# Which transposes go through the DMA crossbar: the folded weights in place of normalised tokens and attention outputs

## The chip, the cores and the metric

The kernel runs on one core of one Trainium2 chip. The metric is the device time of one execution in microseconds. Before the change three executions took 206.52, 206.75 and 206.77 us, a median of 206.75 us.

## The reference

One layer norm feeds two branches, and their outputs are added to the input:

```
xn  = layernorm(x)                       # x: 2048 tokens x 512
q,k,v = split(xn @ wqkv)                 # 32 heads of 16
phi(t) = [softmax(t @ w_phi), softmax(-t @ w_phi)]   # per head, 32 features
kv  = phi(k)^T v ;  z = sum over tokens of phi(k)
o   = (phi(q) kv) / (phi(q) z + 1e-6)
h   = xn @ w1 + b1 ;  act = h * tanh(softplus(h))    # 1792 wide
out = x + o @ wo + act @ w2
```

All tensors are bf16. The attention has no causal mask: kv and z are sums over all tokens, so no o can be made before every token's k and v are done.

## The kernel before, in words

The 2048 tokens are four groups (g) of four tiles (t) of 128 tokens. The width 512 is four blocks of 128 (kt, or j on the head side). TensorE contracts over the partitions, so everything that enters a matmul as a contraction needs its contracted axis on the partitions: the normalised tokens as `xnT` (width on the partitions), the attention output as `oT` (heads on the partitions).

**Loads (lines 69 to 93).** Two queues issue them: ScalarE's queue takes `wk_raw` (L73), `Wsrc` (L77) and `wq_raw` (L81); SyncE's queue takes the first token group in two halves (L71, L74), `wv`, `b1row`, the two halves of `w1_sb` (L86, L87), token group 1 (L89), `w2_sb` (L91) and `wo_sb` (L93). A DMA that ScalarE issues holds ScalarE for the length of the issue. The framework gives DMAs one of eight completion semaphores in turn; a ninth DMA waits, in its queue, for the one that had the semaphore before. L87 is the one that shares with L73.

**Fold (`fold`, L218 to L246).** w_phi is applied to wk and wq once: `wkp = wk @ blockdiag(w_phi)`, and `wqp` likewise. For each of the two, 16 TensorE transposes (L225) put the weight's columns on the partitions in two PSUM banks `ptrw`, two ScalarE copies (L231) take them to `wT`, and 16 small matmuls (L236) against `Wbd` make the folded weight, a bank `pf` for each kt; the banks are copied out by VectorE (L244, even kt) and ScalarE (L246, odd kt).

**Layer norm (`stage_ln`, L166 to L205).** VectorE takes statistics (L178, L179), ScalarE the square root (L182), VectorE the reciprocal (L186) and the normalised tile `xn` (L188). For group 0 TensorE transposes `xn` (L200) into PSUM banks `ptr`, and ScalarE copies them to `xnT` (L204). For groups 1 to 3 the transpose is a DMA (L197) on SyncE's queue, one for each tile, from SBUF to SBUF.

**First loop over the groups (L445 to L462).** `stage_kv_pair`: keys `pk` (L253), two exponentials `ek` (L261, L262), values `pv` (L267), the softmax sums `ss` (L275), reciprocals (L281), and the weighted values `v12` (L283, L291). `stage_q`: queries `pq` (L328), exponentials `eq` (L336, L337), then for each of eight slices a matmul `pS` (L342) and a VectorE product `eqT` (L349). The next group's tokens are loaded (L459) and normalised. `stage_kvacc`: 32 matmuls `pkv` (L303), accumulated by VectorE (L311, L313). `stage_h`: 56 matmuls `ph` (L364) and 14 activations (L374).

**Second loop (L478 to L480).** `stage_o`: for each tile 8 matmuls `pnd` (L388), a reciprocal (L397) and a product `o_t` (L399), which a DMA transpose on SyncE's queue brings into `oT` (L405). `stage_out`: for each tile 14 matmuls with the MLP activations (L415) and 4 with `oT` (L423) in one bank `po`, the addition of x (L431) and the store (L432).

**What sets the order.** Each engine runs its instructions in a fixed order that a scheduler made when the program was built; it interleaves stages (matmuls `ph` fill the time in which VectorE works on the softmax). `chain` fixes the order of ScalarE's activations, and with it the table loads. PSUM has three pools of two buffers: `kq` (pk, pq, ph, pnd), `v` (pv, po), `m` (ptr, ptrw, pf, pS, pkv). The token pool `xg` has two buffers.

Of the kernel before, what the change touches and what calls it, by code (L numbers as in the profile page):

```python
# [8 lines left out]
BF16 = mybir.dt.bfloat16  # L9
# [8 lines left out]
def kernel(  # L18
# [50 lines left out]
    xgs[0] = xpool.tile([P, TPG, D], BF16, name="xg")  # L69
    x0 = x2[0 : TPG * P].rearrange("(t p) d -> p t d", p=P)  # L70
    nc.sync.dma_start(xgs[0][:, 0:2, :], x0[:, 0:2, :])  # L71
    wk_raw = prep_w.tile([P, KT, D], BF16, name="wk_raw")
    nc.scalar.dma_start(wk_raw[:], wqkv_v[:, :, D : 2 * D])  # L73
    nc.sync.dma_start(xgs[0][:, 2:4, :], x0[:, 2:4, :])  # L74
    Wsrc = prep_w.tile([P, 4, DH], BF16, name="Wsrc")
    with nc.allow_non_contiguous_dma(reason="tiny w_phi load"):
        nc.scalar.dma_start(Wsrc[:], wphi_v)  # L77
    wv = wts.tile([P, KT, D], BF16, name="wv")
    nc.sync.dma_start(wv[:], wqkv_v[:, :, 2 * D : 3 * D])
    wq_raw = prep_w.tile([P, KT, D], BF16, name="wq_raw")  # L80
    nc.scalar.dma_start(wq_raw[:], wqkv_v[:, :, 0:D])  # L81
    b1row = prep_w.tile([FT, P], BF16, name="b1row")
    nc.sync.dma_start(b1row[:], b1_v)
    w1_sb = wts.tile([P, KT, F], BF16, name="w1_sb")
# [81 lines left out]
    def stage_ln(g):  # L166
        xg = xgs[g]
        mv = spool.tile([P, TPG, nc.vector.BN_AGGR_DIM], FP32, name="mv")
        rstd = spool.tile([P, TPG], FP32, name="rstd")
        xnT = xnTpool.tile([P, TPG, KT, P], BF16, name="xnT")  # L170
        step = 1 if g == 0 else TPG
        for t0 in range(0, TPG, 2):
            ptr = bank_m("ptr", [P, 2, KT, P], BF16) if g == 0 else None
            for t in range(t0, t0 + 2):
                if t % step == 0:
                    for u in range(t, t + step):
                        st = spool.tile([P, nc.vector.BN_STATS_DIM], FP32, name="st")
                        nc.vector.bn_stats(st[:], xg[:, u, :])  # L178
                        nc.vector.bn_aggr(mv[:, u, :], st[:])  # L179
                    us = slice(t, t + step)  # L180
                    chain(
                        nc.scalar.activation(  # L182
                            rstd[:, us], mv[:, us, 1], ACT.Sqrt, bias=eps_t[:]
                        )
                    )
                    nc.vector.reciprocal(rstd[:, us], rstd[:, us])  # L186
                xn = xnpool.tile([P, D], BF16, name="xn")
                nc.vector.tensor_scalar(  # L188
                    out=xn[:],
                    in0=xg[:, t, :],  # L190
                    scalar1=mv[:, t, 0:1],
                    scalar2=rstd[:, t : t + 1],
                    op0=ALU.subtract,
                    op1=ALU.mult,
                )
                if g > 0:
                    nc.sync.dma_start_transpose(out=xnT[:, t], in_=xn[:])  # L197
                    continue
                for kt in range(KT):
                    nc.tensor.transpose(  # L200
                        ptr[:, t - t0, kt, :], xn[:, kt * P : (kt + 1) * P], ident[:]
                    )
            if g == 0:
                nc.scalar.copy(xnT[:, t0 : t0 + 2], ptr[:])  # L204
        return xnT  # L205


# [7 lines left out]
        op=ALU.mult,  # L215
    )

    def fold(src, dst):  # L218
        wTs = []
        for jh in range(2):  # L220
            ptr = bank_m("ptrw", [P, 2, 512], BF16)
            for jj in range(2):
                j = 2 * jh + jj
                for kt in range(KT):
                    nc.tensor.transpose(  # L225
                        ptr[:, jj, kt * P : (kt + 1) * P],
                        src[:, kt, j * P : (j + 1) * P],
                        ident[:],
                    )
            wT = prep_w.tile([P, 2, 512], BF16, name="wT", bufs=2)  # L230
            nc.scalar.copy(wT[:], ptr[:])  # L231
            wTs.append(wT)
        for kt in range(KT):
            pf = bank_m("pf")
            for j in range(4):
                nc.tensor.matmul(  # L236
                    pf[:, j * P : (j + 1) * P],
                    lhsT=wTs[j // 2][:, j % 2, kt * P : (kt + 1) * P],
                    rhs=Wbd[:, j, :],
                    start=True,  # L240
                    stop=True,
                )
            if kt % 2 == 0:
                nc.vector.tensor_copy(dst[:, kt, :], pf[:])  # L244
            else:
                nc.scalar.copy(dst[:, kt, :], pf[:])  # L246


    def stage_kv_pair(xnT, pr):
        pk = big("pk")  # L250
        for tt in range(2):
            for kt in range(KT):
                nc.tensor.matmul(  # L253
                    pk[:, tt, :],
                    lhsT=xnT[:, 2 * pr + tt, kt, :],
                    rhs=wkp[:, kt, :],
                    start=(kt == 0),
                    stop=(kt == KT - 1),
                )
        ek = ekpool.tile([P, 2, 2, 512], BF16, name="ek")  # L260
        chain(nc.scalar.activation(ek[:, 0], pk[:], ACT.Exp))  # L261
        chain(nc.scalar.activation(ek[:, 1], pk[:], ACT.Exp, scale=-1.0))  # L262
        v12s = []
        for tt in range(2):
            pv = bank_v("pv")
            for kt in range(KT):
                nc.tensor.matmul(  # L267
                    pv[:],
                    lhsT=xnT[:, 2 * pr + tt, kt, :],
                    rhs=wv[:, kt, :],  # L270
                    start=(kt == 0),
                    stop=(kt == KT - 1),
                )
            ss = spool.tile([P, 2, NH], FP32, name="ss")
            nc.vector.reduce_sum(  # L275
                ss[:],
                ek[:, :, tt, :].rearrange("p s (h e) -> p s h e", e=DH),
                axis=AX.X,
            )
            rk = spool.tile([P, 2, NH], FP32, name="rk")  # L280
            nc.vector.reciprocal(rk[:], ss[:])  # L281
            v12 = vpool.tile([P, 2, NH, VW], BF16, name="v12")
            nc.vector.tensor_tensor(  # L283
                out=v12[:, :, :, 0:DH],
                in0=pv[:]
                .rearrange("p (o h e) -> p o h e", o=1, e=DH)
                .to_broadcast([P, 2, NH, DH]),
                in1=rk[:, :, :, None].to_broadcast([P, 2, NH, DH]),
                op=ALU.mult,
            )  # L290
            nc.gpsimd.tensor_copy(v12[:, :, :, DH], rk[:])  # L291
            v12s.append(v12)
        return ek, v12s
# [27 lines left out]
    def stage_q(g, xnT):  # L321
        gs = slice(g * 512, (g + 1) * 512)
        for jp in range(2):
            pq = big("pq")
            for jj in range(2):
                j = 2 * jp + jj
                for kt in range(KT):
                    nc.tensor.matmul(  # L328
                        pq[:, jj, :],
                        lhsT=wqp[:, kt, j * P : (j + 1) * P],  # L330
                        rhs=xnT[:, :, kt, :],
                        start=(kt == 0),
                        stop=(kt == KT - 1),
                    )
            eq = eqpool.tile([P, 2, 2, 512], BF16, name="eq")
            chain(nc.scalar.activation(eq[:, 0], pq[:], ACT.Exp))  # L336
            chain(nc.scalar.activation(eq[:, 1], pq[:], ACT.Exp, scale=-1.0))  # L337
            for jj in range(2):
                j = 2 * jp + jj
                for pl in range(2):  # L340
                    pS = bank_m("pS")
                    nc.tensor.matmul(  # L342
                        pS[:],
                        lhsT=B16b[:],
                        rhs=eq[:, 1 - pl, jj, :],
                        start=True,
                        stop=True,
                    )
                    nc.vector.tensor_tensor(  # L349
                        out=eqT[:, pl * 4 + j, gs],  # L350
                        in0=pS[:],
                        in1=eq[:, pl, jj, :],
                        op=ALU.mult,
                    )


    def stage_h(xnT, pool):
        act = pool.tile([P, FT, 512], BF16, name="act")
        for fp in range(FT // 2):
            ph = big("ph")  # L360
            for ff in range(2):
                f = 2 * fp + ff
                for kt in range(KT):
                    nc.tensor.matmul(  # L364
                        ph[:, ff, :],
                        lhsT=w1_sb[:, kt, f * P : (f + 1) * P],
                        rhs=xnT[:, :, kt, :],
                        start=(kt == 0),
                        stop=(kt == KT - 1),
                    )  # L370
# [8 lines left out]


    def stage_o(g):
        oT = oTpool.tile([P, TPG, 4, P], BF16, name="oT")
        for t in range(TPG):
            tok0 = g * 512 + t * P
            pnd = big("pnd")
# [16 lines left out]
                in1=rd[:, :, :, None].to_broadcast([P, 2, 16, DH]),  # L402
                op=ALU.mult,
            )
            nc.sync.dma_start_transpose(out=oT[:, t], in_=o_t[:])  # L405
        return oT

    def stage_out(g, act, oT):
        xg2 = xpool.tile([P, TPG, D], BF16, name="xg")
        nc.sync.dma_start(xg2[:], x_g[g])  # L410
        for t in range(TPG):
# [10 lines left out]
            for j in range(4):  # L422
                nc.tensor.matmul(  # L423
                    po[:],
                    lhsT=oT[:, t, j, :],
                    rhs=wo_sb[:, j, :],
                    start=False,
                    stop=(j == 3),
# [8 lines left out]
    chain(nc.scalar.activation(warm[:], eps_t[:], ACT.Sqrt))  # L437
    xnTs[0] = stage_ln(0)
    chain(nc.scalar.activation(warm[:], eps_t[:], ACT.Exp))
    fold(wk_raw, wkp)  # L440
    fold(wq_raw, wqp)
    pb = bank_m("pb", [P, FT], BF16)
    nc.tensor.transpose(pb[:], b1row[:], ident[0:FT, 0:FT])
    nc.vector.tensor_copy(b1f[:], pb[:])
# [66 lines left out]
```

## Time and profile before

| what | value |
|---|---|
| median of three executions | 206.75 us |
| the profiled execution | 206.77 us |
| its span in the trace | 205.1 us |
| TensorE matmul busy | 185.3 us |
| VectorE busy | 117.3 us |
| ScalarE busy | 91.4 us |
| granted TensorE clock | 0.999 |

The profile is of one execution. Its span runs from the first to the last instruction; 1.7 us of the execution lie outside. Times in the trace count from the span's start. TensorE's matmuls are pipelined, so that a 128x512 matmul is listed with 379 ns, but eight in a row take 1.73 us; what a matmul costs its queue is the distance to the next, 0.216 us, and not its listed duration. A row for a DMA on a queue shows the time in which the queue was held by the issue; the landing is listed apart.

### The profile page before, as it was taken

The page shows a single profiled execution, that of the slowest core. Times are in us where ns is not written, and L with a number is a line of the kernel's source. Part 1 is how long each engine was busy: PE and PEld are TensorE (multiplying, and loading weights), DVE is VectorE, ACT ScalarE, POOL GpSimd, SP SyncE. Part 2 cuts the span into 40 slices and gives each one's busy share as a digit, 9 for nine tenths or more (in the row PEclk, how much of TensorE's full clock was granted, in tenths as well). Part 3 has the DMA queues.
Part 4 walks back from the last instruction along what each step waited for, and adds up shares of the span by engine and source line. Part 5 has one row for each costly group of instructions (what it writes and reads, how often), then busy time and mean ns, then how long its engine had stood idle before and what let it go on. Part 6 is the DMA issues. An engine that isn't in the chain of part 4 may idle for free.

```text
span 205.1 us, 2739 instructions
## 1 busy us (share of the span) xinstructions
PE 185.3 (90%) x1073; PEld 92.5 (45%) x1073; DVE 117.3 (57%) x205; ACT 91.4 (45%) x119; POOL 8.6 (4%) x25
## 2 busy tenths in 40 slices
PE   0396999999888999989999999999999999999993
PEld 0264443554333644336443446544544464455441
DVE  1807699971999903999309987261372154127211
ACT  2574998448985278994498743600000000000000
POOL 2000011000111000110001100000000000000000
PEclk9999999999999999999999999999999999999999
DMA  5999600084000182000440000053072127103310
GB/s 165 341 372 348 213 0 0 2 80 128 0 2 0 26 94 88 0 0 3 77 128 0 0 3 2 0 102 54 26 198 58 52 69 165 51 29 77 76 51 26
DMA packets 27320, 15.92 MB, mean 78 GB/s; under 512 B 16300, under 2 KB 27308, under 8 KB 27308
## 3 DMA queue, kind: packets, MB, share of 16 engines
q1 hardware_dynamic: 25724, 14.69, 28.0%
q10 hardware_dynamic: 1584, 1.07, 1.8%
q8 instruction: 8, 0.13, 0.2%
q14 instruction: 4, 0.03, 0.1%
HBM read 9.98 MB, written 2.10 MB: 59 GB/s over the span
## 4 chain that ended last, share of the span: by engine, by line
PE 52%; DVE 22%; DMA 13%; ACT 6%; issue 5%; SPq 1%; ACTq 0%
PE po L415 21%; PE ph L364 11%; PE po L423 7%; DMA xg<-in_A_x_dram 7%; DVE eqT L349 5%; DVE ss L275 5%; DMA oT<-o_t 4%; DVE st L178 3%; PE pk L253 3%; PE pv L267 3%; PE pnd L388 2%; DMA wk_raw<-in_A_wqkv_dram 2%; DVE xn L188 2%; ACT ek L262 2%; PE pkv L303 2%
## 5 line engine op out<-in xcount | busy, mean ns | idle before, releaser
L364 PE MATMUL ph<-xnT,w_sb 128*128 128x512 bf16 x224 | 55.0, 379 | 0.5 <-ACT act L374 0.5
L415 PE MATMUL po<-w_sb,act 128*128 128x512 bf16 x224 | 52.4, 379 | 0.0
L374 ACT ACTIVATE act<-ph,b1f 128x512 bf16<-128x512 f32 x56 | 35.2, 684 | 27.5 <-PE ph L364 27.5
L431 DVE TENSOR_TENSOR y<-po,xg 128x512 bf16<-128x512 f32 x16 | 11.1, 692 | 43.4 <-PE po L423 43.3
L364 PEld LDWEIGHTS <-w_sb 128*128 128x128 bf16 x224 | 21.6, 98 | 27.2 <-issue 3.1
L415 PEld LDWEIGHTS <-act 128*128 128x128 bf16 x224 | 21.5, 98 | 23.6
L275 DVE TENSOR_REDUCE ss<-ek 128x64 f32<-128x1024 bf16 x16 | 18.7, 1200 | 16.7 <-ACT ek L262 16.7
L349 DVE TENSOR_TENSOR eqT<-pS,eq 128x512 bf16<-128x512 f32 x32 | 20.5, 685 | 1.1 <-PE pS L342 0.9
L178 DVE BATCH_NORM_STATS2 st<-xg 128x6 f32<-128x512 bf16 x16 | 10.4, 673 | 15.1 <-DMA xg<-in_A_x_dram 15.1
L267 PE MATMUL pv<-wv,xnT 128*128 128x512 bf16 x64 | 16.6, 385 | 1.4 <-DVE v_594 L283 1.4
L423 PE MATMUL po<-wo_sb,oT 128*128 128x512 bf16 x64 | 16.5, 379 | 0.9 <-DMA oT<-o_t 0.9
L328 PE MATMUL pq<-xnT,wqp 128*128 128x512 bf16 x64 | 15.1, 379 | 1.6 <-ACT ek L262 1.5
L253 PE MATMUL pk<-wkp,xnT 128*128 128x512 bf16 x64 | 15.8, 379 | 0.0
L342 PE MATMUL pS<-eq,B16b 128*128 128x512 bf16 x32 | 11.6, 378 | 1.1 <-DVE eqT L349 1.1
L399 DVE TENSOR_TENSOR o_t<-pnd,rd 128x512 bf16<-128x512 f32 x16 | 11.1, 692 | 0.5
L328 PEld LDWEIGHTS <-wqp 128*128 128x128 bf16 x64 | 6.2, 97 | 9.7 <-issue 2.8
L267 PEld LDWEIGHTS <-xnT 128*128 128x128 bf16 x64 | 6.3, 100 | 8.5 <-issue 1.9
L423 PEld LDWEIGHTS <-oT 128*128 128x128 bf16 x64 | 6.0, 98 | 9.1 <-DMA oT<-o_t 2.2
L388 PEld LDWEIGHTS <-eqT 128*128 128x128 bf16 x128 | 8.2, 98 | 3.8 <-DVE o_t L399 2.3
L200 PE MATMUL ptr<-ident,xn 128*128 128x128 bf16 x16 | 2.0, 311 | 8.7 <-DVE xn L188 8.7
L388 PE MATMUL pnd<-kvm,eqT 128*128 128x136 bf16 x128 | 9.6, 223 | 0.0
L261 ACT ACTIVATE ek<-pk 128x1024 bf16<-128x1024 f32 x8 | 8.2, 1029 | 2.3 <-ACT ek L262 2.1
(99 smaller groups left out, 171.6 us busy)
## 6 DMA issues: line engine op xcount, KB each, us to landing
xg<-in_A_x_dram SPq DMA_DIRECT2D x7, 512.0 KB, 3.8
out_dram<-y SPq DMA_DIRECT2D x16, 128.0 KB, 1.7
w_sb<-in_B_w_dram SPq DMA_DIRECT2D x2, 896.0 KB, 9.1
w_sb<-in_B_w_dram SPq DMA_DIRECT2D x1, 1792.0 KB, 14.7
wk_raw<-in_A_wqkv_dram ACTq DMA_DIRECT2D x1, 512.0 KB, 4.8
xg<-in_A_x_dram SPq DMA_DIRECT2D x2, 256.0 KB, 4.4
wv<-in_A_wqkv_dram SPq DMA_DIRECT2D x1, 512.0 KB, 7.5
wq_raw<-in_A_wqkv_dram ACTq DMA_DIRECT2D x1, 512.0 KB, 8.4
```

The lines of the kernel that those rows point to most:

```text
L178: nc.vector.bn_stats(st[:], xg[:, u, :])
L253: nc.tensor.matmul(pk[:, tt, :], lhsT=xnT[:, 2 * pr + tt, kt, :], rhs=wkp[:, kt, :], start=(kt == 0), stop=(kt == KT - 1),)
L267: nc.tensor.matmul(pv[:], lhsT=xnT[:, 2 * pr + tt, kt, :], rhs=wv[:, kt, :], start=(kt == 0), stop=(kt == KT - 1),)
L275: nc.vector.reduce_sum(ss[:], ek[:, :, tt, :].rearrange("p s (h e) -> p s h e", e=DH), axis=AX.X,)
L328: nc.tensor.matmul(pq[:, jj, :], lhsT=wqp[:, kt, j * P : (j + 1) * P], rhs=xnT[:, :, kt, :], start=(kt == 0), stop=(kt == KT - 1),)
L342: nc.tensor.matmul(pS[:], lhsT=B16b[:], rhs=eq[:, 1 - pl, jj, :], start=True, stop=True,)
L349: nc.vector.tensor_tensor(out=eqT[:, pl * 4 + j, gs], in0=pS[:], in1=eq[:, pl, jj, :], op=ALU.mult,)
L364: nc.tensor.matmul(ph[:, ff, :], lhsT=w1_sb[:, kt, f * P : (f + 1) * P], rhs=xnT[:, :, kt, :], start=(kt == 0), stop=(kt == KT - 1),)
L374: nc.scalar.activation(act[:, f, :], ph[:, ff, :], ACT.Mish, bias=b1f[:, f : f + 1])
L388: nc.tensor.matmul(pnd[:, j // 2, (j % 2) * 136 : (j % 2) * 136 + 136], lhsT=eqT[:, pl * 4 + j, tok0 : tok0 + P], rhs=kvm[:, pl * 4 + j, : ...
L415: nc.tensor.matmul(po[:], lhsT=act[:, f, ts], rhs=w2_sb[:, f, :], start=(f == 0), stop=False,)
L423: nc.tensor.matmul(po[:], lhsT=oT[:, t, j, :], rhs=wo_sb[:, j, :], start=False, stop=(j == 3),)
```

## The change

The crossbar transposes move from the activations to the weights. `wkT` and `wqT` are loaded already transposed, each by one DMA transpose of 512x512 from DRAM on ScalarE's queue, in the place where `wk_raw` and `wq_raw` were loaded. `fold` keeps only its matmuls and the copies of `pf`. The tiles of groups 1 to 3 are now transposed as those of group 0 were: 16 TensorE transposes a group into two banks of the pool `m`, and two ScalarE copies of 128x1024. The attention output likewise: 16 TensorE transposes a group into two banks `ptro` of the same pool, and two ScalarE copies into `oT`. The layouts of `xnT` and `oT` change from (tile, block, 128) to (block, 512).

```diff
-    nc.scalar.dma_start(wk_raw[:], wqkv_v[:, :, D : 2 * D])
+    wkT = prep_w.tile([P, 4, D], BF16, name="wkT")
+    nc.scalar.dma_start_transpose(out=wkT[:], in_=A_wqkv[:, D : 2 * D])
...
-    nc.scalar.dma_start(wq_raw[:], wqkv_v[:, :, 0:D])
+    wqT = prep_w.tile([P, 4, D], BF16, name="wqT")
+    nc.scalar.dma_start_transpose(out=wqT[:], in_=A_wqkv[:, 0:D])
...
         for t0 in range(0, TPG, 2):
-            ptr = bank_m("ptr", [P, 2, KT, P], BF16) if g == 0 else None
+            ptr = bank_m("ptr", [P, KT, 2 * P], BF16)
...
-                if g > 0:
-                    nc.sync.dma_start_transpose(out=xnT[:, t], in_=xn[:])
-                    continue
                 for kt in range(KT):
                     nc.tensor.transpose(
-                        ptr[:, t - t0, kt, :], xn[:, kt * P : (kt + 1) * P], ident[:]
-                    )
-            if g == 0:
-                nc.scalar.copy(xnT[:, t0 : t0 + 2], ptr[:])
+                        ptr[:, kt, (t - t0) * P : (t - t0 + 1) * P],
+                        xn[:, kt * P : (kt + 1) * P],
+                        ident[:],
+                    )
+            nc.scalar.copy(xnT[:, :, t0 * P : (t0 + 2) * P], ptr[:])
...
-    def fold(src, dst):
-        wTs = []
-        for jh in range(2):
-            ptr = bank_m("ptrw", [P, 2, 512], BF16)
...
-            wT = prep_w.tile([P, 2, 512], BF16, name="wT", bufs=2)
-            nc.scalar.copy(wT[:], ptr[:])
-            wTs.append(wT)
+    def fold(wT, dst):
...
-            nc.sync.dma_start_transpose(out=oT[:, t], in_=o_t[:])
+            o_ts.append(o_t)
+        for jh in range(2):
+            ptr = bank_m("ptro", [P, 2, 512], BF16)
+            for t in range(TPG):
+                for jj in range(2):
+                    j = 2 * jh + jj
+                    nc.tensor.transpose(
+                        ptr[:, jj, t * P : (t + 1) * P],
+                        o_ts[t][:, j * P : (j + 1) * P],
+                        ident[:],
+                    )
+            nc.scalar.copy(oT[:, 2 * jh : 2 * jh + 2, :], ptr[:])
```

## The prediction

> **What bounds the kernel now.** First the page's head and its first part, then the chain of waits in order of time, to see where TensorE sets the pace and where something else does.
>
> ```profile
> span 205.1 us, 2739 instructions
> PE 185.3 (90%) x1073; PEld 92.5 (45%) x1073; DVE 117.3 (57%) x205; ACT 91.4 (45%) x119; POOL 8.6 (4%) x25
> PE   0396999999888999989999999999999999999993
> ```
>
> TensorE is busy almost throughout, except in the first four slices (20 us). The chain tells which parts are TensorE's. In it, columns are start, length, and work:
>
> ```profile
> 6.02 10.00 DMA xg<-in_A_x_dram
> 16.04 0.69 DVE st L178
> ...
> 18.63 0.46 PE ptrw L225 x8
> ...
> 23.67 1.22 DVE ss L275
> ...
> 46.69 3.53 DMA xg<-in_A_x_dram
> 50.24 1.29 DVE st L178 x2
> ...
> 75.48 1.73 PE pk L253 x8
> ```
>
> Two DMA arrivals hold VectorE: token group 1 at 16.04 us, and token group 3 at 50.24 us, whose load stands in SyncE's queue behind the four crossbar transposes of group 1 (held 40.68 to 46.64 by the timeline). Eight matmuls of 512 columns take 1.73 us, 0.216 each; eight warm transposes take 0.46, 0.058 each. From the timeline the stages are: start to the first softmax sum `ss` 23.67 us; from there to group 1's first `pk` at 46.09, 22.42; group 1 to 75.31, 29.22; group 2 to 102.92, 27.61; group 3 to 130.91, 27.99; outputs to 201.67, 70.76; tail 3.40. Their sum is 205.07.
>
> TensorE's work in a group is 112 x 0.216 + 32 x 0.06 (`pkv`) = 26.1 us, in an output group 72 x 0.216 + 32 x 0.058 (`pnd`) = 17.4. So group 2 has 1.5 us of gaps, group 1 3.1, the four output groups together 2 (the first lacks four `po`, done earlier). The extra 1.6 of group 1 is VectorE's late statistics: `ss` comes 4.75 us after `pk` in group 2, 6.9 in group 1.
>
> **What the Trainium skill says.** "Perfetto Trace Analysis", Per-instruction lifecycle (HWDGE): the slot of a DMA on its queue is descriptor generation; moving the data is not in it. The trace agrees:
>
> ```profile
> L405 SPq DMA_TRANSPOSE oT<-o_t x16: 1189/1208/1225, 132.5 to 189.8; - x16
> DMA to landing us min/median/max: 2.4/2.4/3.9
> ```
>
> The queue is held 1.21 us, the data land 2.4 us after the issue. "DMA: Bandwidth & Descriptors", Latency and other measured facts, gives 261 GB/s for a crossbar transpose: 2.0 us for one 512 KB weight. The trace has no transpose from DRAM; from SBUF its 256-byte packets took 18 ns (median), so 16 engines need 2048 x 18 / 16 = 2.3 us, against 1.5 for 512 packets of 1024 bytes at 46 ns. I take 2.3. "TensorE: Matmul & The Clock Gate", Part 4, gives about 275 ns for a transpose in context; here 219 is what one lasts, 0.058 us what one costs in a row; the measurement decides.
>
> ```profile
> L225 PE MATMUL ptrw<-ident,wq_raw 128*128 128x128 bf16 x16 | 1.1, 219 | 0.0
> L204 ACT COPY xnT<-ptr 128x1024 bf16<-128x1024 bf16 x2 | 1.9, 1004 | 0.0
> L423 PE MATMUL po<-wo_sb,oT 128*128 128x512 bf16 x64 | 16.5, 379 | 0.9 <-DMA oT<-o_t 0.9
> ```
>
> The last row shows what the removed transposes of `o_t` cost TensorE: 0.9 us in all.
>
> **The change part by part.** TensorE loses 32 transposes and gains 48 + 64: +80 x 0.058 = +4.6 us on an engine that is nearly full. What the rest adds or gives back, stage by stage:
>
> *Start.* Gone are 32 transposes (1.9 us) and four ScalarE copies (4 x 1.0), which lie on the chain. But in the built program VectorE's order is `wkp` twice, then the first statistics of group 1, then `wqp`. VectorE waits there for group 1's tokens, and TensorE's later `pf`, the eighth `pk` and `ek` wait for `wqp`'s bank. Counting on: statistics 0.69, `wqp` 0.69, `pf` and last `pk` about 0.6, ScalarE's last `wqp` copy 0.6, two `ek` 2.05, with hand-overs: `ss` starts 4.8 us after the tokens land. They land at 16.04 now. The two weights cost the DMA engines 2 x (2.3 - 1.5) = 1.6 us more ahead of them, and the second half of `w1_sb`, which stands ahead of them in the queue, waits for `wkT`:
>
> ```profile
> SPq L87 <- DMA wk_raw<-in_A_wqkv_dram: 2.3, 1, 2.3
> ```
>
> I take a landing at 17.6 to 18, so `ss` at 22.6.
>
> The other limit is ScalarE's issue. Not shown: what a 512x512 transpose from DRAM holds. Low bound: a plain load's 0.49 us, and ScalarE is free at 2.45 as now. High bound: four times 1.21, twice, from 0.81, with `Wsrc` between: free at 11.1. Behind it stand the square roots of group 0. From a free ScalarE to `ss` I count 12.0 us: table load 1.28, four roots with VectorE's `xn` to 3.8, transposes to 4.2, two copies to 5.9 (after the second table load), then the `pf` banks, two at a time, each through a copy of 0.6 to 0.7: `wqp` done at 9.9, two `ek` 2.05. That gives `ss` at 14.5 or 23.1. The later limit decides: 22.6 to 23.1. I take 22.7, 1.0 earlier than now.
>
> *Group 0, from `ss`.* In the built program it has the order that group 2 has now, where `ss` to next `pk` takes 102.92 - 80.06 = 22.9. Added: 16 transposes 0.93; VectorE's one statistics of group 2 before `xn`, 0.2 of its 0.69 after cover by `ph`; and waits in pool `m`: `pkv`'s banks must wait for ScalarE's copies of `ptr` (2 x 1.0 after the eighth transpose), of which the remaining transposes and three `ph` hide all but 0.5. 24.5 us, +2.1. Without that `ph` cover the copies would cost about 1.1 more.
>
> *Group 1.* Group 2's 27.6 + 0.93 + 0.5 = 29.0: -0.2. The 1.6 goes, since group 3's load no longer stands behind transposes: it issues when group 1's `xn` are done (about 40) and lands 3.8 later, ahead of its statistics. What is late next is `ek`, as in group 2.
>
> *Group 2.* The same sum, 29.0: +1.4. *Group 3* has no transposes: 0.
>
> ScalarE's copies (2.0 a group) lie in its waits for `ph` (27.5 us over the loop). The copies of `oT` fall where ScalarE has nothing: its slices are zero from 133 us on.
>
> *Outputs.* 64 x 0.058 = +3.7. The 0.9 of waits for DMA goes. Transposes of `o_t` wait for VectorE, but in places where `pnd` waited for the same `o_t` already, so they fill about 0.2 a group. New: the fourth tile's transposes end, ScalarE copies `ptro` twice (2.0), while TensorE has five `po`, two `po` with `oT`, two `po`: 1.9. About 0.3 a group stays. Sum 3.7 - 0.9 - 0.6 + 1.2 = +3.4. If the nine matmuls did not cover the copies, each group would lose 1.9 more.
>
> SyncE's queue is only relieved: 28 transposes leave it, and stores and loads behind them go earlier; no one waits for those.
>
> Sum: -1.0 + 2.1 - 0.2 + 1.4 + 0 + 3.4 = +5.7, span 210.8. The profiled execution took 206.77 for a span of 205.1, so 1.7 lie around it, and it is 0.02 above the median: 212.5 us.
>
> **The rivals.**
> *(a) The crossbar load is slow from DRAM.* Twice 18 ns per packet is 9.2 us of all engines for both weights instead of 3.0 in the plain loads: tokens of group 1 at 22.2, `ss` at 27.0, 4.3 later than forecast: 216.8 us. For it: one packet of a queue takes its turn against one of the other, and the transposed weight comes in four times as many. Against it: the engines have only 3.4 MB to bring in that time.
> *(b) The start gains more and the banks cost nothing.* Landing at 16.04, `ss` at 20.9 (-1.8), no waits in pool `m` (-1.5), 0.6 less in the outputs: 208.6 us. Still slower: the transposes are TensorE work.
> *(c) Faster.* All stages after the first sum to +6.7, so the change wins only if `ss` starts before 23.67 - 6.7 = 17.0 us, that is if the tokens of group 1 land before 12.2. With a landing at 10, `ss` at 14.8 and 204.6 us. For it: ScalarE and TensorE alone would be ready at 14.5 (low bound above). Against it: the tokens stand behind both halves of `w1_sb` in SyncE's queue, which the change doesn't reorder.
> That the change doesn't do what it says is excluded by the built program: no `ptrw`, 112 transposes elsewhere.
>
> **How the numbers follow.** Forecast (210 to 214.5) 0.62, (a) 0.2, (b) 0.11, (c) 0.04, a cancellation within 0.2% 0.03. Within 0.2% is about what a measurement of this kernel can tell from no change. The range reaches from between (b) and the forecast, 209.2, to just over (a), 217.0; outside lie half of (b), (c), and issues slower than bounded. Faster 0.04, same 0.03, slower 0.93.
>
> **What would show it.** Rows for transposes: `ptr` 64, `ptro` 64, 0.058 us apart. Start: the first `ss` at 22.6 to 23.1; tokens of group 1 at 17.6 to 18; the issues on ScalarE's queue between 0.5 and 4.8 us each. Group 1: `ss` within 5 us of its `pk`, no wait of VectorE for tokens. Groups 1 and 2 equal, near 29.0. Outputs near 74.2 with no wait for DMA. Wrong would be: `ss` at 27 or before 21, ScalarE held by the loads beyond 11 us, or TensorE waiting for copies by more than 0.5 us a group.

## The result, and the profile after

The changed kernel takes 213.0 us (median of four executions, 212.22 to 213.06) where the kernel before takes 206.76 (206.52 to 206.78): a ratio of 1.0296, with a 95% interval of 1.0271 to 1.0321. The change makes the kernel about 6 us slower. The forecast was 212.5 us. The profiled execution took 212.96 us for a span of 211.2.

The head of the page of the changed kernel, with the totals and two rows of the forty slices (5.3 us each):

```profile
span 211.2 us, 2838 instructions
PE 190.3 (90%) x1153; PEld 95.7 (45%) x1153; DVE 118.0 (56%) x205; ACT 100.4 (48%) x129; POOL 8.5 (4%) x25
PE   0039998999999999989999999999999999999993
ACT  0085798569895868976689734430030003002100
```

TensorE's busy time grew by 5.0 us, its share is still 90%: the span grew with it. ScalarE's row was this before:

```profile
ACT  2574998448985278994498743600000000000000
```

ScalarE, which had work from the first slice on, now has none in the first two, and has bursts at the end, where it copies `ptro`.

Cut at the same points as in the prediction (group 3 and the outputs at the first `pnd` of the second loop), the two traces give, in us:

| stage | before | predicted | after | after minus before |
|---|---|---|---|---|
| start to first `ss` | 23.67 | 22.7 | 24.14 | +0.47 |
| group 0, from `ss` | 22.42 | 24.5 | 24.05 | +1.63 |
| group 1 | 29.22 | 29.0 | 28.74 | -0.48 |
| group 2 | 27.61 | 29.0 | 28.74 | +1.13 |
| group 3 | 27.83 | 28.0 | 27.82 | 0 |
| outputs | 70.94 | 74.2 | 74.35 | +3.41 |
| tail | 3.41 | 3.4 | 3.36 | 0 |

All stages but the first are within 0.5 us of the forecast, and the sum of the differences is +6.1. The first is the one that failed: a gain of 1.0 us was forecast, and none came. The chain of waits of the changed kernel in order of time (start, length, work):

```profile
...
3.45 16.00 DMA wqT<-in_A_wqkv_dram
19.50 0.40 PE pf L220 x4
...
41.21 0.54 PE ptr L197 x8
...
45.11 3.24 PE ph L350 x15
48.35 1.73 PE pk L238 x8
...
52.94 2.36 DVE ss L261 x2
```

No token group stands in this chain any more: group 1's `ss` follows its `pk` by 4.6 us without a DMA between, where the chain of before had the load of group 3. In its place the start hangs on the crossbar load of the query weight, 16.0 us from issue to landing. The timeline of the changed kernel shows what that load did to ScalarE (start, length, queue or engine, work, and in brackets what the engine waited for):

```profile
0.80 1.39 ACTq L73 DMA_TRANSPOSE wkT<-in_A_wqkv_dram  x1
2.22 1.20 ACTq L77 DMA_DIRECT2D Wsrc<-in_A_w_phi_dram  x1
3.45 7.91 ACTq L81 DMA_TRANSPOSE wqT<-in_A_wqkv_dram  x1
...
11.39 1.28 ACT L435 ACT_TABLE_LOAD   x1 [11.39 <-issue]
12.80 0.83 ACT L182 ACTIVATE rstd<-mv,eps_t 128x1 f32<-128x1 f32 x4
...
13.78 1.98 PE L197 MATMUL ptr<-ident,xn 128*128 128x128 bf16 x16 [13.78 <-DVE xn L188]
...
19.50 0.40 PE L220 MATMUL pf<-Wbd,wqT 128*128 128x128 bf16 x4 [0.21 <-DMA wqT<-in_A_wqkv_dram]
...
24.14 1.22 DVE L261 TENSOR_REDUCE ss<-ek 128x64 f32<-128x1024 bf16 x1 [0.31 <-ACT ek L247]
```

The first crossbar issue held ScalarE's queue for 1.39 us, the second, of the same size, for 7.91. So ScalarE starts on its table load and group 0's square roots at 11.39 us instead of 2.45, and TensorE's first transposes wait for them until 13.78. The chain names the landing of `wqT` because it came last, but the wait for it is only 0.21 us: two limits, the landing and ScalarE's late start, fall almost together.

The groups of transposes and the rows that stand for the removed waits (op, count, then busy time, mean ns, and the idle time before with its releaser):

```profile
L197 PE MATMUL ptr<-ident,xn 128*128 128x128 bf16 x64 | 6.1, 243 | 13.8 <-DVE xn L188 13.8
L398 PE MATMUL ptro<-ident,o_t 128*128 128x128 bf16 x64 | 6.2, 219 | 0.0
L403 ACT COPY oT<-ptro 128x1024 bf16<-128x1024 bf16 x8 | 7.7, 1015 | 53.5 <-PE ptro L398 53.5
L421 PE MATMUL po<-wo_sb,oT 128*128 128x512 bf16 x64 | 17.2, 380 | 0.0
```

`po` waited 0.9 us for the transposes by DMA before, and waits for nothing now; the 53.5 us in which ScalarE waits for `ptro` lie where it has no other work. The waits view has what came in their place (in all, times, longest):

```profile
PEld L421 <- ACT oT L403: 3.2, 8, 0.5
...
PEld L289 <- ACT xnT L202: 1.3, 3, 0.5
```

These are waits of the weight loads, not of the matmuls; in the chain of the second output group two pairs of `po` with `oT` take 0.52 and 0.48 us instead of 0.43, so that most of the 3.2 us costs nothing.

### The profile page after: what moved, and what is told of

Its sections match the earlier page's. It is cut to its first block, busy times and chain, and to the rows that moved or that the text cites. A ratio compares the mean times of both kernels' runs of the same rounds, so it can differ in the third digit from the quotient of the medians.

```text
span 211.2 us, 2838 instructions
## 1 busy us (share of the span) xinstructions
PE 190.3 (90%) x1153; PEld 95.7 (45%) x1153; DVE 118.0 (56%) x205; ACT 100.4 (48%) x129; POOL 8.5 (4%) x25
## 3 DMA queue, kind: packets, MB, share of 16 engines
q10 hardware_dynamic: 4688, 1.07, 3.0%
## 4 chain that ended last, share of the span: by engine, by line
PE 73%; ACT 12%; DMA 8%; DVE 4%; ACTq 1%; issue 1%
PE po L413 23%; PE ph L350 18%; DMA wqT<-in_A_wqkv_dram 8%; PE po L421 7%; PE pk L238 4%; PE pkv L289 4%; PE pnd L375 4%; PE pv L253 4%; DVE ss L261 3%; PE pS L328 3%; PE pq L314 3%; ACT eq L323 2%; ACT ek L247 2%; ACT L360 2%; ACT L182 2%; ACT act L360 2%
## 5 line engine op out<-in xcount | busy, mean ns | idle before, releaser
L350 PE MATMUL ph<-xnT,w_sb 128*128 128x512 bf16 x224 | 55.7, 379 | 1.7 <-ACT act L360 1.7
L413 PE MATMUL po<-w_sb,act 128*128 128x512 bf16 x224 | 54.4, 379 | 0.0
L429 DVE TENSOR_TENSOR y<-po,xg 128x512 bf16<-128x512 f32 x16 | 11.1, 692 | 46.8 <-PE po L421 46.8
L403 ACT COPY oT<-ptro 128x1024 bf16<-128x1024 bf16 x8 | 7.7, 1015 | 53.5 <-PE ptro L398 53.5
L197 PE MATMUL ptr<-ident,xn 128*128 128x128 bf16 x64 | 6.1, 243 | 13.8 <-DVE xn L188 13.8
L421 PE MATMUL po<-wo_sb,oT 128*128 128x512 bf16 x64 | 17.2, 380 | 0.0
L314 PE MATMUL pq<-xnT,wqp 128*128 128x512 bf16 x64 | 15.1, 379 | 1.4 <-ACT ek L247 1.4
L197 PEld LDWEIGHTS <-xn 128*128 128x128 bf16 x64 | 4.5, 108 | 15.5 <-DVE xn L188 14.9
L386 DVE TENSOR_TENSOR o_t<-pnd,rd 128x512 bf16<-128x512 f32 x16 | 11.1, 692 | 0.6
```

Of the source, the lines that this page charges most:

```text
L314: nc.tensor.matmul(pq[:, jj, :], lhsT=wqp[:, kt, j * P : (j + 1) * P], rhs=xnT[:, kt, :], start=(kt == 0), stop=(kt == KT - 1),)
L350: nc.tensor.matmul(ph[:, ff, :], lhsT=w1_sb[:, kt, f * P : (f + 1) * P], rhs=xnT[:, kt, :], start=(kt == 0), stop=(kt == KT - 1),)
L386: nc.vector.tensor_tensor(out=o_t[:].rearrange("p (a h e) -> p a h e", a=2, e=DH), in0=nd[:, :, :, 0:DH], in1=rd[:, :, :, None].to_broadca ...
L413: nc.tensor.matmul(po[:], lhsT=act[:, f, ts], rhs=w2_sb[:, f, :], start=(f == 0), stop=False,)
L421: nc.tensor.matmul(po[:], lhsT=oT[:, j, ts], rhs=wo_sb[:, j, :], start=False, stop=(j == 3),)
```

## The experiments

The theory: the price is TensorE's transposes, in groups 0 to 2 and in the outputs, and the start gives nothing back because ScalarE is held while it issues the second crossbar load. The rivals: the start is set by the landings (of the query weight, or of group 1's tokens), whoever issues; or one of the three parts carries the loss alone. The runs were made in three lots, each on another chip with executions of the kernel before beside them. On all three chips the kernel before was slower than the 206.76 above (medians 208.5, 208.59 and 208.29), so the ratios below are against that; the stages come from the traces. The kernel before was traced in the first comparison only, so a stage "before" is always that one trace.

### Plain loads in the changed kernel

```diff
-    nc.scalar.dma_start_transpose(out=wkT[:], in_=A_wqkv[:, D : 2 * D])
+    nc.scalar.dma_start(wkT[:], wqkv_v[:, :, D : 2 * D])
...
-    nc.scalar.dma_start_transpose(out=wqT[:], in_=A_wqkv[:, 0:D])
+    nc.scalar.dma_start(wqT[:], wqkv_v[:, :, 0:D])
```

> The changed kernel with its two weight loads as plain DMAs of the same size; the weights then go into the folds untransposed, so that part of the computation is left out, and every instruction order but the two loads is that of the changed kernel. Theory (ScalarE is held by the crossbar issues, and the transposed weight and group 1's tokens land late, all of it the price of the crossbar loads): ScalarE free at 2.5 us, group 1's tokens at about 16, first softmax sum at about 20.9 instead of 24.1, the later stages as in the changed kernel (24.1, 28.7, 28.7, 27.8, 74.3): span 208.0, 209.7 us. Rival (the start is bound by the chain of roots, xn, pf and pk, whatever the loads do): first softmax sum still at 24, 213.0 us.

Measured: 209.29 us, ratio 1.0015 (0.9994 to 1.0035), `ss` at 20.42 us, and every later stage as in the changed kernel (24.05, 28.73, 28.74, 27.82, 74.33). From the timeline of this run:

```profile
1.89 0.53 ACTq L81 DMA_DIRECT2D wqT<-in_A_wqkv_dram  x1
2.44 1.28 ACT L435 ACT_TABLE_LOAD   x1 [2.44 <-issue]
...
16.20 0.69 DVE L178 BATCH_NORM_STATS2 st<-xg 128x6 f32<-128x512 bf16 x1 [2.06 <-DMA xg<-in_A_x_dram]
...
20.42 1.22 DVE L261 TENSOR_REDUCE ss<-ek 128x64 f32<-128x1024 bf16 x1
```

Without the crossbar the removal of 32 transposes and four copies is worth 23.67 - 20.42 = 3.25 us of the start; the two crossbar loads cost 24.14 - 20.42 = 3.7. These differences hold to a few tenths: in the five traces in which the start was that of the kernel before, `ss` came at 23.67 to 24.03. With ScalarE free at 2.44 the limit is the one that the prediction named first: tokens land at 16.2, `ss` comes 4.2 later.

### One part at a time

The three parts of the diff, each alone in the kernel before: the weights' loads and `fold`; `stage_ln` with the layout of `xnT`; `stage_o` with the layout of `oT`. The diffs are the parts of the one shown in the section on the change.

> The kernel before with only the two weight loads through the crossbar. Theory: first softmax sum at 24.1 as in the changed kernel, later stages as before: 205.8 span, 207.4 us, so that taking 32 transposes and four copies away gains nothing. Rival (those 1.9 us of TensorE and 4 us of ScalarE are gained, and the loads are hidden): first softmax sum at 21, 204 us.

> The kernel before with only the normalised tokens of groups 1 to 3 transposed by TensorE. Theory, stage by stage: 23.7, 24.1, 28.7, 28.7, 27.8, outputs 70.9 as before, tail 3.4: span 207.3, 209.0 us. Rival (the loop's transposes lie beside VectorE's work and cost nothing, all the loss is in the outputs): 206.8 us, or 205.2 if group 1's late statistics also go.

> The kernel before with only the attention outputs transposed by TensorE. Theory: 64 transposes of 0.058 us less the waits for DMA plus waits for the copies of ptro, outputs 74.3 instead of 70.9, all else as before: 210.2 us. Rival (the transposes fill the waits for o_t and for the crossbar): 208 us or less.

| stage | before | weights alone | tokens alone | outputs alone | all three |
|---|---|---|---|---|---|
| start to `ss` | 23.67 | 25.59 | 24.03 | 23.81 | 24.14 |
| group 0 | 22.42 | 22.92 | 23.69 | 22.41 | 24.05 |
| group 1 | 29.22 | 28.22 | 29.05 | 30.98 | 28.74 |
| group 2 | 27.61 | 27.61 | 28.73 | 27.61 | 28.74 |
| outputs | 70.94 | 72.38 | 73.61 | 74.34 | 74.35 |
| time, us | | 209.67 | 211.01 | 211.39 | |
| ratio | | 1.0021 | 1.0105 | 1.0114 | 1.0296 |
| 95% | | 0.9995 to 1.0046 | 1.005 to 1.0159 | 1.0059 to 1.0168 | 1.0271 to 1.0321 |

(The first and last columns are from the first comparison.) No part carries the loss alone. The tokens cost group 0 1.3 us and group 2 1.1; the transposes of `o_t` cost the outputs 3.4; the weights cost the start 1.9, with ScalarE held 8.49 us and TensorE waiting 0.8 us for `wqT` to land. What was expected came in group 2 of the tokens (28.7) and in the outputs of `o_t` (74.3); it did not come in the start of the weights alone (24.1 expected, 25.59), and the times of the last two kernels are 2.0 and 1.2 us above those expected. Two kinds of stages were not touched by a part and still moved. Outputs with the DMA transposes took 72.38 and 73.61 us in two of these traces, with waits of `po` for `oT` of 2.3 and 3.4 us, against 70.94 and 0.9 in the first trace of before. And group 1 of the outputs-alone kernel, whose tokens go through the crossbar as before, took 30.98. (The traces of the last two kernels are of executions of 212.05 and 212.53 us, 1.0 and 1.1 above their medians.) Its timeline:

```profile
40.81 6.46 SPq L197 DMA_TRANSPOSE xnT<-xn  x4
...
47.33 0.57 SPq L471 DMA_DIRECT2D xg<-in_A_x_dram  x1
51.24 1.29 DVE L178 BATCH_NORM_STATS2 st<-xg 128x6 f32<-128x512 bf16 x2 [6.02 <-DMA xg<-in_A_x_dram]
```

The tokens of group 3 are asked for only when the queue is through with its four transposes, at 47.33, and VectorE waits 6.0 us for them. So the stages that hang on the crossbar transposes vary from trace to trace; of those without, group 2 with transposes on TensorE took 28.73 or 28.74 in every trace that had them.

### The changed kernel again, with the load later, and with the tokens first

Three runs on one chip: the changed kernel once more; the same with the crossbar load of wq issued after group 0's square roots; and the same with group 1's tokens asked for ahead of the two halves of `w1_sb`.

```diff
-    nc.scalar.dma_start_transpose(out=wqT[:], in_=A_wqkv[:, 0:D])
...
     xnTs[0] = stage_ln(0)
+    chain(nc.scalar.dma_start_transpose(out=wqT[:], in_=A_wqkv[:, 0:D]))
```

```diff
+    xgs[1] = xpool.tile([P, TPG, D], BF16, name="xg")
+    nc.sync.dma_start(xgs[1][:], x_g[1])
     nc.sync.dma_start(w1_sb[:, :, 0:F2], w1_v[:, :, 0:F2])
     nc.sync.dma_start(w1_sb[:, :, F2:F], w1_v[:, :, F2:F])
-    xgs[1] = xpool.tile([P, TPG, D], BF16, name="xg")
-    nc.sync.dma_start(xgs[1][:], x_g[1])
```

> The changed kernel once more, to stand beside the others of this call on one chip. Theory: from the first softmax sum on, its stages are 24.05, 28.74, 28.74, 27.82, 74.35 as in its first profile, since no transfer but the start's is on its path; only the start may move with the chip, and the kernel before may move by more, since its crossbar transposes and group 3's tokens are on its path: a ratio of 1.020 to 1.030. Rival (the chip sets one factor for both): 1.030 again.

> The changed kernel with the query weight's crossbar load issued by ScalarE after the four square roots instead of ahead of them. Theory (the hold of ScalarE is only one of three limits that end together; the query weight's slow landing is the next): roots done at about 8.5 us instead of 13.6, the weight lands at 19 to 20 all the same, first softmax sum at 24 to 24.7, time within 0.3% of the changed kernel. Rival (the hold alone delayed the start): first softmax sum at 21 to 21.5, 210 us.

> The changed kernel with token group 1 loaded ahead of both halves of w1. Theory: the tokens land at about 12 instead of 18.8, VectorE's statistics no longer wait, but ScalarE's hold to 11.4 and the query weight's landing at about 19 stay: first softmax sum at 23.8 to 24.2, same time as the changed kernel. Rival (the tokens set the start, 4.8 us before the first softmax sum): 21 or earlier, 210 us.

| run | time, us | ratio, 95% | `ss` at | ScalarE held by wq | wq issued, landed | tokens of group 1 landed |
|---|---|---|---|---|---|---|
| changed kernel again | 212.96 | 1.0188 (1.0159 to 1.0218) | 23.70 | 7.45 | 3.59, 18.6 | 17.8 |
| wq later | 214.88 | 1.0292 (1.0251 to 1.0332) | 25.00 | 5.13 | 7.89, 20.3 | 15.2 |
| tokens first | 213.15 | 1.0202 (1.0162 to 1.0241) | 23.74 | 6.32 | 3.59, 15.4 | 10.6 |
| changed kernel, first comparison | 213.0 | 1.0296 (1.0271 to 1.0321) | 24.14 | 7.91 | 3.45, 19.45 | 18.75 |

The stages after `ss` agree with the first trace of the changed kernel to 0.2 us or better in all three, as was expected of the repeat; its ratio lies at the lower edge of the 1.020 to 1.030 expected. The repeat and the run with the tokens first part the limits. In the repeat, TensorE took `wqT` without a wait; it had landed just before, at 18.6:

```profile
3.59 7.45 ACTq L81 DMA_TRANSPOSE wqT<-in_A_wqkv_dram  x1
...
11.06 1.28 ACT L435 ACT_TABLE_LOAD   x1 [11.06 <-issue]
...
18.88 0.39 PE L220 MATMUL pf<-Wbd,wqT 128*128 128x128 bf16 x4
...
23.70 2.35 DVE L261 TENSOR_REDUCE ss<-ek 128x64 f32<-128x1024 bf16 x2 [0.32 <-ACT ek L247]
```

From the table load to `ss` are 12.64 us here and 12.75 in the first trace. (The chain view of the repeat names the second half of `w1_sb` as what the first `pf` waits for, though `pf` does not read it. That wait ends 1.05 us after ScalarE's first copy of `ptr` began, as the first wait behind that copy does, at 1.04 to 1.05, in four traces that name the copy.) With the tokens first, the tokens landed 7 us earlier than in the repeat and the query weight 3 us earlier, but `ss` came no earlier. The chain of that run shows no landing ahead of `ss`:

```profile
0.79 1.39 ACTq L73
2.22 1.35 ACTq L77
3.59 6.32 ACTq L81
9.94 1.28 ACT L435
...
23.74 2.34 DVE ss L261 x2
```

It is ScalarE's hold, then the table load, and the chain of group 0. ScalarE was free 1.1 us earlier than in the repeat, and that gain was lost again: VectorE, which had the tokens early, took two of group 1's statistics ahead of the mask product `Wbd`, and TensorE waited for it:

```profile
15.30 0.58 PE L220 MATMUL pf<-Wbd,wkT 128*128 128x128 bf16 x4 [1.00 <-DVE Wbd L207]
```

The late load is the other case: the roots ran at 5 to 8 us, but then ScalarE was held anyway, ahead of its second table load and the copies of `ptr`, and the weight landed at 20.3:

```profile
7.89 5.13 ACTq L436 DMA_TRANSPOSE wqT<-in_A_wqkv_dram  x1
13.05 1.28 ACT L437 ACT_TABLE_LOAD   x1 [4.87 <-issue]
20.39 0.46 PE L219 MATMUL pf<-Wbd,wqT 128*128 128x128 bf16 x4 [0.47 <-DMA wqT<-in_A_wqkv_dram]
```

Moving the issue behind the roots lengthened the start: 0.9 us later than in the first trace, and 1.3 later than in the repeat. I had expected a time within 0.3% of the changed kernel's, and that was a miss (0.9% longer than the repeat): I had not counted that the copies stand behind the issue, too, nor that the weight lands later.

### The crossbar load on the other queue

The changed kernel with wq's crossbar load on SyncE's queue, behind group 1's tokens, both ahead of `w1_sb`.

```diff
-    nc.scalar.dma_start_transpose(out=wqT[:], in_=A_wqkv[:, 0:D])
...
+    xgs[1] = xpool.tile([P, TPG, D], BF16, name="xg")
+    nc.sync.dma_start(xgs[1][:], x_g[1])
+    wqT = prep_w.tile([P, 4, D], BF16, name="wqT")
+    nc.sync.dma_start_transpose(out=wqT[:], in_=A_wqkv[:, 0:D])
     w1_sb = wts.tile([P, KT, F], BF16, name="w1_sb")
```

> The changed kernel with the query weight's crossbar load taken from ScalarE's queue and put into SyncE's, behind group 1's tokens, both ahead of w1. Theory (ScalarE's hold by the second crossbar issue decides the changed kernel's start): ScalarE is free at about 2.5 instead of 11.4, the query weight lands by 14 or so, and the first softmax sum comes at 18 to 20 instead of 24.1; the other stages as in the changed kernel, so 4 to 6 us less than it, 207 to 209 us. Rival (the landing of the crossbar load decides, whichever queue issues it): it lands at 19 or later again, the sum comes at 23 to 25, and the time stays within 1 us of the changed kernel's 213.

Measured: 211.86 us, ratio 1.0154 (1.0118 to 1.019), `ss` at 21.25. ScalarE was free at 3.6, the weight landed at 12.2. From its timeline:

```profile
3.59 1.28 ACT L435 ACT_TABLE_LOAD   x1 [3.59 <-issue]
...
7.14 2.99 SPq L85 DMA_TRANSPOSE wqT<-in_A_wqkv_dram  x1
...
10.48 1.29 DVE L178 BATCH_NORM_STATS2 st<-xg 128x6 f32<-128x512 bf16 x2 [0.76 <-DMA xg<-in_A_x_dram]
...
12.50 0.59 PE L220 MATMUL pf<-Wbd,wkT 128*128 128x128 bf16 x4 [2.11 <-DVE Wbd L207]
```

The direction is the theory's and against the rival's: the hold is gone, the weight lands in time, and the start is 2.5 to 2.9 us shorter than in the two traces of the changed kernel. The closest comparison is the run with the tokens first, which differs in the queue of this one load: there `wqT` had landed long before its use, and `ss` came at 23.74. The size is not: I had said 18 to 20 and 207 to 209 us. Two terms failed. VectorE waited for group 1's tokens (10.48) ahead of the mask product `Wbd`, and TensorE waited 2.11 us for that; and group 0 became 25.90 instead of 24.05, with another order of `pk` and `pv` on TensorE and a wait of ScalarE of 2.3 us for `pq`. Once ScalarE is out of the way, the tokens and the order of the fold are the next limit. The load could not start at once either: SyncE waited 3.6 us until `wkT` had landed. That agrees with the Trainium skill, "DMA: Bandwidth & Descriptors", Rules for kernel authors, which has two DMA transposes from different queues serialised by a wait for the first.

### The load of group 3 in the kernel before

The prediction put group 1's excess in the kernel before, 1.6 us, on group 3's load behind the crossbar transposes. Two ways to take it out of that place: GpSimd issues it, or a third token buffer lets it be issued at the start (with one `ek` buffer fewer for the room).

```diff
-                nc.sync.dma_start(xgs[g + 1][:], x_g[g + 1])
+                (nc.sync if g + 1 == 2 else nc.gpsimd).dma_start(xgs[g + 1][:], x_g[g + 1])
```

> The kernel before with one edit: token group 3 is loaded by GpSimd's queue, so that it doesn't stand behind the crossbar transposes of group 1. Theory: the statistics of group 3 are done before the first ek of group 1, group 1's stage falls from 29.2 to 27.6, a ratio of 0.992 against the kernel before. Rival (VectorE or the exponentials hold group 1 anyway): 29.2 as before, ratio 1.000.

```diff
-    xpool = ctx.enter_context(tc.tile_pool(name="xg", bufs=2))
+    xpool = ctx.enter_context(tc.tile_pool(name="xg", bufs=3))
...
-    ekpool = ctx.enter_context(tc.tile_pool(name="ek", bufs=3))
+    ekpool = ctx.enter_context(tc.tile_pool(name="ek", bufs=2))
```

> The kernel before with a third token buffer (and two instead of three ek buffers), so that group 3's tokens are asked for at the start and no load stands behind the crossbar transposes of group 1. Theory (group 1's extra 1.6 us in the kernel before is the queueing of that load): group 1 goes from 29.2 to 27.6 us as group 2 has it, the other stages stay, and the time falls by 1.6 us, ratio about 0.992 to the kernel before. Rival (the crossbar transposes themselves, or the scheduler's order, hold group 1 back): group 1 stays at 29 us or more and the time within 0.2%.

GpSimd: 208.06 us, ratio 0.9986 (0.996 to 1.0011), group 1 at 29.16, a miss. Three buffers: 205.1 us, ratio 0.983 (0.9796 to 0.9864), group 1 at 27.61. The timeline of the first shows why it failed:

```profile
40.95 6.48 SPq L197 DMA_TRANSPOSE xnT<-xn  x4
42.19 0.87 POOL L459 DMA_DIRECT2D xg<-in_A_x_dram  x1 [7.93 <-DVE xn L188]
...
48.56 1.29 DVE L178 BATCH_NORM_STATS2 st<-xg 128x6 f32<-128x512 bf16 x2 [3.21 <-DMA xg<-in_A_x_dram]
48.76 1.04 PE L253 MATMUL pk<-wkp,xnT 128*128 128x512 bf16 x4 [1.38 <-DMA xnT<-xn]
```

The load was issued 4.5 us earlier than in the kernel before, but now it ran beside the transposes: it needed over 6 us instead of 3.5, and TensorE waited 1.38 us for a transposed tile. That the two held each other up on the DMA engines would explain it; no run parts this from GpSimd's loads being slower in themselves. With three buffers no load runs beside the transposes, and group 1 takes the 27.61 us of group 2:

```profile
40.89 5.70 SPq L197 DMA_TRANSPOSE xnT<-xn  x4
...
47.05 0.66 DVE L178 BATCH_NORM_STATS2 st<-xg 128x6 f32<-128x512 bf16 x1
51.53 2.34 DVE L275 TENSOR_REDUCE ss<-ek 128x64 f32<-128x1024 bf16 x2 [3.60 <-ACT ek L262]
```

So the claim on the queue stands for group 1: VectorE waits for `ek` and no longer for tokens. (The edit also takes one `ek` buffer away; no run separates the two.) The time fell by more than expected: on its own chip by 3.2 us, twice the 1.6, a ratio of 0.983 where 0.992 was expected. Only against the first comparison's 206.76, on another chip, is it 1.6. Without a trace of the kernel before on this chip, where the rest lies is not shown; the outputs, at 70.67, are shorter than in the traces of two other kernels that keep both the DMA transposes and two token buffers (71.9 and 71.7, GpSimd's and the one with the tokens first below).

### Group 1's tokens first in the kernel before, with three buffers and with two

With three buffers and group 1's tokens ahead of `w1_sb`; and with the tokens ahead alone (edits as shown above).

> As the run with three token buffers, and the load of group 1's tokens moved ahead of the two halves of w1. Theory: in the kernel before the first softmax sum waits for these tokens (they land at 16.0, the sum comes at 23.7); with a landing near 10 the chain through ScalarE, TensorE and VectorE decides, and the sum comes 1 to 2 us earlier; with the gain of group 1 a time 2.6 to 3.6 us below the kernel before, ratio 0.983 to 0.988. Rival: the start has a second limit just behind (the w1 halves now land later and the first ph wait for them), so that it gains nothing and the ratio is that of the run with three buffers alone.

> The kernel before with only the load of group 1's tokens moved ahead of the two halves of w1. Theory: the first softmax sum 1 to 2 us earlier, all else as before: ratio 0.990 to 0.995. Rival: w1 lands later and gives it back within group 0: ratio 0.998 to 1.002.

Both edits: 204.22 us, ratio 0.9791 (0.9755 to 0.9827), `ss` at 23.07, group 1 at 27.61; it is the fastest version. On its own chip that is 4.1 us below the kernel before, more than the 2.6 to 3.6 expected; the start came 0.6 earlier than in the first trace of before, less than the 1 to 2 expected. Tokens first alone: 207.14 us, ratio 0.9934 (0.9914 to 0.9954), as expected; `ss` at 21.73, but group 1, which was to stay at 29.2, at 30.83. Why `ss` is 1.3 us later with both edits than with one was not taken apart: TensorE's order in the fold differs between them. The best arrangement with transposes on the crossbar is thus 7.6 us below the best with transposes on TensorE that was tried (211.86, same chip).

## Why the prediction was right, step by step

The forecast of 212.5 us came within 0.5 of the measured 213.0, and part of that closeness is luck: the start was taken 1.4 us too short, groups 0 to 2 together 1.0 us too long. The mechanism of the loss was right, that of the start was not.

**TensorE's transposes.** Right, and most of the loss. 64 `ptr` and 64 `ptro` are in the trace. In group 1's stretch of the chain 16 of them take 0.85 + 0.22 = 1.07 us (0.93 counted), and the page's busy time of TensorE grew by 5.0 (4.6 counted), of the 6.1 by which the span grew.

**Start** (predicted -1.0, measured +0.47). This step failed. The prediction weighed two limits and took 22.7, close to the landing of group 1's tokens plus 4.8. The other limit decided, at the high bound of its unknown: "twice, from 0.81, with `Wsrc` between: free at 11.1", then 12.0 us to `ss`, 23.1. Measured: free at 11.36, and from the table load at 11.39 another 12.75 us. That the bound came out was luck: the two issues took 1.39 and 7.91 us in place of twice 4.84. The tokens landed at 18.75 where 17.6 to 18 was taken, and nobody waited for them. The prediction had listed "ScalarE held by the loads beyond 11 us" as a sign that it was wrong; here it was. What it had as to the plain part was right: with plain loads `ss` came 4.2 us after the tokens, and the gain was 3.25 us. The crossbar loads took it back. Whether they took more than that is not shown: `ss` came at 24.14 and 23.70 with the change, and at 23.67 to 24.03 in five traces with the start of before.

**Group 0** (predicted +2.1, measured +1.63). The base of 22.9, read off group 2, was right: with the weights alone, which put no transposes into the group, it took 22.92. The transposes then add 24.05 - 22.92 = 1.13, where 0.93 + 0.2 + 0.5 = 1.63 was counted. That 22.42 + 1.63 is also 24.05 is chance.

**Group 1** (predicted -0.2, measured -0.48) **and group 2** (+1.4, +1.13). That group 1's old excess was the load is shown by the run with three buffers. The sum was 0.3 too high in both, and the term that was mis-sized is the wait for the copies of `ptr`: of the 1.13 us that group 2 gained, 1.07 are the transposes' own time on the chain, so that next to nothing is left for the 0.5. The weight loads of `pkv` do wait for the copies, 1.3 us in three groups and 0.5 at most, but in the chain the `pkv` of these groups follow without a gap worth naming.

**Outputs** (predicted +3.4, measured +3.41). Right to the sum: the 64 `ptro` take 3.72 us of the chain (3.7 counted), the DMA waits are gone, and the cover of the copies by nine matmuls held: a `po` pair lost 0.1 us at most in the second output group. The run with this part alone has the same 74.34 us. Two reservations: 0.2 a group for four groups is 0.8, where the prediction took off 0.6; and the 3.41 are against the 70.94 of one trace, while with DMA transposes the outputs took 70.67 to 73.61 us in the traces of this case.

**Rivals.** (a), the slow landing, came halfway: `wqT` did land at 19.45, 16.0 us after its issue, but the wait for it was 0.21 us; it stands in the chain of the run with the late issue and of the weights alone. Its reason did not come: (a) had the two weights take 6.2 us more of all DMA engines than the plain loads, and by the pages the packets of ScalarE's queue took 3.0% of the span after and 1.8% before, 6.3 and 3.7 us, so 2.6 more. (b) was half right: the waits in pool `m` came to almost nothing, but the start did not gain. (c) needed `ss` before 17.0, and no run came near: the earliest was 20.42.

**The size in other runs.** The loss is 3.0% in the first comparison and 1.9% in the repeat on another lot's chip (1.0159 to 1.0218). It is the kernel before that differs, 206.76 and 208.59; the changed one takes 213.0 on both. Three buffers alone bring the 23 executions between 207.57 and 209.43 down to four between 205.04 and 205.13, with all 28 crossbar transposes left in, so the excess is not the transposes' alone: it goes when group 3's load no longer stands behind them in SyncE's queue (with one `ek` buffer fewer, as said). In the trace of that run the outputs, too, are at 70.67. What differs between the chips stays open.

## What to carry to other kernels

A transpose that the DMA does beside a full TensorE saves a slot there (0.058 us here) as long as its landing is hidden; moving it onto TensorE costs that slot every time, and waits for DMAs that look large in a view may be worth little (of the 15.1 us in which VectorE waited for tokens in the kernel before, 5.2 fell into group 1, and they were worth 1.6). Before a DMA is put on an engine's own queue, look at what that engine has to do next: a second crossbar load cost ScalarE 6 to 8.5 us ahead of the square roots with which everything starts. And where a load stands behind other DMAs of a queue, ask for it earlier rather than from another queue: here a third buffer took the 1.6 us away, and GpSimd's queue did not.

## What the runs showed of the hardware that was not expected

**An issue can hold its queue for several times as long as an equal one.** The first crossbar load of 512x512 held ScalarE's queue 1.39 us or 1.40 us in every trace, the second 7.91, 7.45, 8.49, 6.32 and 5.13 us, and 2.99 on SyncE's queue before `w1_sb` was asked for. It is not only crossbar loads: of two plain loads of 512 KB on SyncE's queue, the one issued first and the one issued last, the second was held sixteen times as long in the run with plain loads:

```profile
1.80 0.46 SPq L79 DMA_DIRECT2D wv<-in_A_wqkv_dram  x1
...
8.18 7.38 SPq L93 DMA_DIRECT2D wo_sb<-in_A_wo_dram  x1
```

The Trainium skill, "Perfetto Trace Analysis", Per-instruction lifecycle (HWDGE), puts a wait for the lock on the descriptor generator and the generation itself into that slot; the loads compared have the same size, so generation alone does not explain the difference. What else was in flight is the likely cause; no run took it apart further. That the first crossbar load was still under way is not enough of an explanation: in the run with the late issue `wkT` had landed at 6.6, and the issue at 7.89 still held ScalarE 5.13 us.

**The same load lands in 5.1 or 16.0 us.** The Trainium skill, "DMA: Bandwidth & Descriptors", Latency and other measured facts, has 261 GB/s; an estimate from that figure is 2.0 us for 512 KB, and no landing here was that short. On SyncE's queue, ahead of `w1_sb`, the landing took 5.1 us; on ScalarE's queue, beside `w1_sb`, 16.0. The view of the DMA from 9 to 14 us in the changed kernel (queue, packets, MB, share of 16 engines; q1 is SyncE's, q10 ScalarE's):

```profile
q1 hardware_dynamic: 537, 0.93, 83.8%
q10 hardware_dynamic: 938, 0.24, 28.3%
```

The crossbar's packets are 256 bytes, SyncE's here 1.7 KB on average. 938 packets in 5 us are 188 per us; at that rate the 2048 of one weight need 10.9 us. The same page, Rules for kernel authors, says that DMAs of two issuing engines are interleaved on the same 16 engines; the trace agrees in so far as both queues moved packets in these 5 us. The small packets get 0.24 of 1.17 MB. In the same 5 us of the kernel before, whose loads are plain, the engines moved 1.88 MB, and in the three other traces that have the second crossbar load in flight from 3.6 us on 0.85 to 1.41: the crossbar load did not only get a small part, all queues together moved less. In the run with the late issue it was 1.80.
